# An attention block, forward and backward: the key cache read once instead of twice, through a per-head V^T(e·K), and the work around it rescheduled

## The chip, the cores and the metric

The kernel runs on one core of one Trainium2 chip. The metric is the device time of one execution in microseconds (us). The engines are called by the names that the profile uses: PE (TensorE, matrix products; PEld is its weight load), DVE (VectorE), ACT (ScalarE), POOL (GpSimd) and SP (SyncE, which here only issues DMA).

## The reference

One transformer block with an adaptive layer norm, for a single decoded token per batch entry, and its full vector-Jacobian product. Batch is 2, there are 32 heads, so 64 (batch, head) pairs, called heads below. All data is bf16.

```python
# per head: q is one vector of 128; K and V are 8192 x 128
scores = einsum('bhqd,bhkd->bhqk', q, k_cache) * Dh ** -0.5
p = softmax(scores)
o = einsum('bhqk,bhkd->bhqd', p, v_cache)
x = x + ga * (o @ wo)                     # then layer norm, SwiGLU FFN (512 -> 1376 -> 512), residual
...
_out, _vjp = jax.vjp(_f, A_x, A_k_cache, A_v_cache, A_wq, A_wo, B_w1, B_w3, B_w2, c, w_mod)
return (_out, *_vjp(grad_out))
```

What matters is the size of things. K and V hold 134.2 MB each (64 heads of 2.10 MB), and their gradients dK and dV are as large. With one query per head, the gradients are outer products:

- dV[k,:] = p[k] · dO, and dK[k,:] = ds[k] · q · scale, where dP[k] = V[k,:] · dO, ds[k] = p[k] · (dP[k] − σ) and σ = o · dO.
- dq = scale · Σ ds[k] · K[k,:].

dO is known only after every head's output has gone through the output projection, the FFN and back. So any scheme has at least two passes over the heads: one before the FFN, one after.

## The kernel before

It makes three passes over caches. Pass 1 reads K: 64 transposes and 64 one-column products per head give the scores of all heads. Then one batched softmax in fp32. Pass 2 reads V: 64 one-column products per head give o. After the FFN, pass 3 reads V and K again, one head after another:

```python
def c_load(i):
    d["v"] = vpool2.tile([P, KK, P], BF16, name="v2")           # two buffers
    nc.sync.dma_start(d["v"][:], A_v_cache[b, h]...)
    d["k"] = kpool2.tile([P, KK, P], BF16, name="k2")           # one buffer
    nc.sync.dma_start(d["k"][:], A_k_cache[b, h]...)
# ... cut: c_prep_dp transposes V (64 blocks, evicted by ACT) and gets DP = V dO, 64 one-column products
def c_finish(i):
    nc.vector.scalar_tensor_tensor(dscs32[:], DP_ps[:], SIG32[:, h, b:b + 1], p32, ALU.subtract, ALU.mult)
    # ... cut
    for kk in range(KK):                                        # KK = 64 rows of 128 per partition
        nc.vector.tensor_scalar(dk_sb[:, kk, :], Qb[:], dscs32[:, kk:kk + 1], None, ALU.mult)
        if kk % 8 in (1, 4, 7):
            nc.scalar.activation(dv_sb[:, kk, :], DOb[:], ACT.Copy, scale=p32[:, kk:kk + 1])
        else:
            nc.vector.tensor_scalar(dv_sb[:, kk, :], DOb[:], p32[:, kk:kk + 1], None, ALU.mult)
    nc.gpsimd.dma_start(out_2[b, h]..., dk_sb[:])
    nc.scalar.dma_start(out_3[b, h]..., dv_sb[:])
    for kk in range(KK):                                        # dq, the only reason to read K again
        nc.tensor.matmul(misc[:, 2 * P:2 * P + 1], k_sb[:, kk, :], dscs_bf[:, kk:kk + 1],
                         start=(kk == 0), stop=(kk == KK - 1))
```

The gradients of the weights follow as a tail of their own.

Of the kernel before, what the change touches and what calls it, by code (L numbers as in the profile page):

```python
# [12 lines left out]
AX = mybir.AxisListType  # L13
EPS = 1e-5
# [3 lines left out]
def kernel(  # L18
# [29 lines left out]
    assert Sq == 1  # L48
# [9 lines left out]
    NBH = B * H  # L58
    SCL = float(Dh) ** -0.5
    GRP = 8  # L60
    assert KK % GRP == 0
    NSD = 0
    NSP = KK - NSD
    NGA = NSP // GRP
    NGC = KK // GRP
# [3 lines left out]

    cst = ctx.enter_context(tc.tile_pool(name="cst", bufs=1))  # L70
    cols = ctx.enter_context(tc.tile_pool(name="cols", bufs=1))
    estp = ExitStack()
    tpsum = estp.enter_context(tc.tile_pool(name="tpsum", bufs=3, space=bass.MemoryType.PSUM))
# [3 lines left out]
    identf = cst.tile([P, P], F32, name="identf")  # L77
    masks.make_identity(nc, identf[:])
    onesf = cst.tile([P, P], F32, name="onesf")
    nc.vector.memset(onesf[:], 1.0)  # L80
    eps_t = cst.tile([P, 1], F32, name="eps_t")
    nc.vector.memset(eps_t[:], EPS)

    P32_all = cst.tile([P, NBH, KK], F32, name="P32_all")
    O32 = cst.tile([P, H, B], F32, name="O32")
    O_bf = cst.tile([P, H, B], BF16, name="O_bf")
    qT32 = cst.tile([P, H, B], F32, name="qT32")
    qT_bf = cst.tile([P, H, B], BF16, name="qT_bf")
    DO32 = cst.tile([P, H, B], F32, name="DO32")
    DO_bf = cst.tile([P, H, B], BF16, name="DO_bf")  # L90
    DQ32 = cst.tile([P, H, B], F32, name="DQ32")
    DQ_bf = cst.tile([P, H, B], BF16, name="DQ_bf")
    SIG32 = cst.tile([P, H, B], F32, name="SIG32")
    wqT_bf = cst.tile([P, H, D], BF16, name="wqT_bf")
    wmT_bf = cst.tile([P, MC, D], BF16, name="wmT_bf")
# [3 lines left out]

    x_col = col("x_col")  # L100
    c_col = col("c_col")
    dy_col = col("dy_col")
    sigc_col = col("sigc_col")
    sc_col = col("sc_col")
    sc_col_bf = col("sc_col_bf", NC, BF16)
    dslc_col = col("dslc_col")
    mod_col = col("mod_col", MC)
    mean1 = col("mean1", 1)
    rstd1 = col("rstd1", 1)
    xn1_col = col("xn1_col")  # L110
    h1_col = col("h1_col")
    h1_col_bf = col("h1_col_bf", NC, BF16)
    attn_col = col("attn_col")
    x1_col = col("x1_col")
    mean2 = col("mean2", 1)
    rstd2 = col("rstd2", 1)
    xn2_col = col("xn2_col")
    h2_col = col("h2_col")
    h2_col_bf = col("h2_col_bf", NC, BF16)
    gate_col = col("gate_col", FC)  # L120
    up_col = col("up_col", FC)
    sigg_col = col("sigg_col", FC)
    sg_col = col("sg_col", FC)
    hh_col = col("hh_col", FC)
    hh_col_bf = col("hh_col_bf", FC, BF16)
    dsl_col = col("dsl_col", FC)
    ffn_col = col("ffn_col")
    x2_col = col("x2_col")
    d_gb_col = col("d_gb_col")
    d_ffn_col = col("d_ffn_col")  # L130
    d_ffn_col_bf = col("d_ffn_col_bf", NC, BF16)
    d_hh_col = col("d_hh_col", FC)
    d_gate_col = col("d_gate_col", FC)
    d_gate_col_bf = col("d_gate_col_bf", FC, BF16)
    d_up_col = col("d_up_col", FC)
    d_up_col_bf = col("d_up_col_bf", FC, BF16)
    d_h2_col = col("d_h2_col")
    d_cb_col = col("d_cb_col")
    d_xn2_col = col("d_xn2_col")
    d_x1_col = col("d_x1_col")  # L140
    d_ga_col = col("d_ga_col")
    d_attn_col = col("d_attn_col")
    d_attn_col_bf = col("d_attn_col_bf", NC, BF16)
    d_h1_col = col("d_h1_col")
    d_ca_col = col("d_ca_col")
    d_xn1_col = col("d_xn1_col")
    d_x0_col = col("d_x0_col")
    d_mod_col = col("d_mod_col", MC)
    d_mod_col_bf = col("d_mod_col_bf", MC, BF16)
    d_sc_col = col("d_sc_col")  # L150
    d_c_col = col("d_c_col")

    for t_ in (gate_col, up_col, d_hh_col):
        nc.vector.memset(t_[:], 0.0)

    def dram_row_to_col(dram2d, dst_col, wrk, cvt_pool):
        rowb = wrk.tile([B, D], BF16, name="rowb")
        nc.scalar.dma_start(rowb[:], dram2d)
        row32 = wrk.tile([B, D], F32, name="row32")
        nc.vector.tensor_copy(row32[:], rowb[:])  # L160
        ps = cvt_pool.tile([P, NC, B], F32, name="colps", tag="vps")
        for kc in range(NC):
            nc.tensor.transpose(ps[:, kc, :], row32[:, kc * P:(kc + 1) * P], identf[:B, :B])
        nc.scalar.copy(dst_col[:], ps[:])

    def col_to_row_bf(src_col, nch, sizes, row_pool, ps_pool, name):
        assert src_col.dtype == F32
        row = row_pool.tile([B, nch * P], BF16, name=name, tag=name)
        per = 4
        for c0 in range(0, nch, per):  # L170
            cn = min(per, nch - c0)
            ps = ps_pool.tile([B, per * P], F32, name="rowps", tag="rowps")
            for i in range(cn):
                fs = sizes[c0 + i]
                nc.tensor.transpose(ps[:, i * P:i * P + fs], src_col[:fs, c0 + i, :], identf[:fs, :fs])
            width = (cn - 1) * P + sizes[c0 + cn - 1]
            nc.vector.tensor_copy(row[:, c0 * P:c0 * P + width], ps[:, :width])
        return row

    def ln_forward(x_in_col, xn_out, mean_t, rstd_t, wrk, psum_pool):  # L180
        ps = psum_pool.tile([P, NC, B], F32, name="lnps", tag="vps")
        nc.tensor.matmul(ps[:], onesf[:], x_in_col[:], start=True, stop=True)
        s1 = wrk.tile([P, 1, B], F32, name="ln_s1")
        nc.vector.tensor_reduce(s1[:, 0, :], ps[:].rearrange("p kc b -> p b kc"), AX.X, ALU.add)
        nc.scalar.mul(mean_t[:], s1[:], 1.0 / D)
        xc = wrk.tile([P, NC, B], F32, name="ln_xc")
        nc.vector.tensor_tensor(xc[:], x_in_col[:], mean_t[:].to_broadcast((P, NC, B)), ALU.subtract)
        sq = wrk.tile([P, NC, B], F32, name="ln_sq")
        nc.vector.tensor_mul(sq[:], xc[:], xc[:])
        ps2 = psum_pool.tile([P, NC, B], F32, name="lnps2", tag="vps")  # L190
        nc.tensor.matmul(ps2[:], onesf[:], sq[:], start=True, stop=True)
        s2 = wrk.tile([P, 1, B], F32, name="ln_s2")
        nc.vector.tensor_reduce(s2[:, 0, :], ps2[:].rearrange("p kc b -> p b kc"), AX.X, ALU.add)
        std = wrk.tile([P, 1, B], F32, name="ln_std")
        nc.scalar.activation(std[:], s2[:], ACT.Sqrt, bias=eps_t[:], scale=1.0 / D)
        nc.vector.reciprocal(rstd_t[:], std[:])
        nc.vector.tensor_mul(xn_out[:], xc[:], rstd_t[:].to_broadcast((P, NC, B)))

    def ln_backward(g_col, xn_col, rstd_t, out_col, wrk, psum_pool, add_col=None):
        gx = wrk.tile([P, NC, B], F32, name="lnb_gx")  # L200
        nc.vector.tensor_mul(gx[:], g_col[:], xn_col[:])
        both = wrk.tile([P, NC, 2, B], F32, name="lnb_both")
        nc.vector.tensor_copy(both[:, :, 0, :], g_col[:])
        nc.vector.tensor_copy(both[:, :, 1, :], gx[:])
        ps = psum_pool.tile([P, NC, 2, B], F32, name="lnbps", tag="vps")
        nc.tensor.matmul(ps[:], onesf[:], both[:], start=True, stop=True)
        ss = wrk.tile([P, 1, 2, B], F32, name="lnb_ss")
        nc.vector.tensor_reduce(ss[:, 0, :, :], ps[:].rearrange("p kc t b -> p t b kc"), AX.X, ALU.add)
        nc.scalar.mul(ss[:], ss[:], 1.0 / D)
        t1 = wrk.tile([P, NC, B], F32, name="lnb_t1")  # L210
        nc.vector.tensor_tensor(t1[:], g_col[:], ss[:, :, 0, :].to_broadcast((P, NC, B)), ALU.subtract)
        t2 = wrk.tile([P, NC, B], F32, name="lnb_t2")
        nc.vector.tensor_mul(t2[:], xn_col[:], ss[:, :, 1, :].to_broadcast((P, NC, B)))
        nc.vector.tensor_tensor(t1[:], t1[:], t2[:], ALU.subtract)
        nc.vector.tensor_mul(out_col[:], t1[:], rstd_t[:].to_broadcast((P, NC, B)))
        if add_col is not None:
            nc.vector.tensor_add(out_col[:], out_col[:], add_col[:])

    esq = ctx.enter_context(ExitStack())
    kpool = esq.enter_context(tc.tile_pool(name="kpool", bufs=3))  # L220
    heads = [(b, h) for b in range(B) for h in range(H)]
    NHD = len(heads)
    k_tiles = {}

    def k_load(i):
        b, h = heads[i]
        k_tiles[i] = kpool.tile([P, KK, P], BF16, name="k_sb")
        nc.sync.dma_start(k_tiles[i][:], A_k_cache[b, h].rearrange("(p kk) d -> p kk d", p=P))
# [7 lines left out]
    for i in range(min(3, NHD)):  # L236
        k_load(i)
# [534 lines left out]
```

## Time and profile before

The first four runs had a median of 2263.3 us (2243.78 to 2266.1). The profiled execution spans 2262.2 us. First, lines of the page of the kernel before: busy time of each engine with its share of the span, then the span in 40 slices (a digit is the busy share in tenths; PEclk is the granted TensorE clock; GB/s is what the DMA engines moved).

```profile
...
PE 1344.2 (59%) x26590; PEld 1192.6 (53%) x26590; DVE 1408.7 (62%) x7399; ACT 1341.3 (59%) x2847; POOL 35.2 (2%) x72
...
DVE  1444444620000058888788788788788788788775
...
PEclk9999999865555566556656656565656665656555
DMA  6999999579999849999999999999999999999975
GB/s 279 353 357 352 359 354 356 225 293 416 426 425 424 367 184 410 409 407 384 413 398 390 400 400 382 407 407 395 403 393 397 402 400 392 410 388 404 401 279 233
DMA packets 72041, 841.19 MB, mean 372 GB/s; under 512 B 7535, under 2 KB 18491, under 8 KB 21563
...
```

No engine is above 62%, and DMA is near full in most slices. But averages over stages hide limits, so the table by stage matters more. Next, the windows view of the kernel before: for each stretch its length, the busy time of PE, PEld, DVE, ACT and POOL (with instruction counts), the PE clock, the DMA share and GB/s.

```profile
...
25.00:415.00 390.00, 355.76 (x8190) 342.50 (x8191) 181.53 (x301) 256.20 (x291) 0.00 (x0) 1.00 0.90 341
415.00:520.00 105.00, 62.11 (x1226) 56.79 (x1224) 43.86 (x75) 40.57 (x71) 0.00 (x0) 0.66 0.67 257
520.00:790.00 270.00, 101.48 (x3482) 97.00 (x3480) 13.82 (x81) 12.59 (x81) 0.00 (x0) 0.50 0.98 415
790.00:845.00 55.00, 42.91 (x802) 39.42 (x799) 25.45 (x130) 22.28 (x50) 0.00 (x0) 0.62 0.52 193
845.00:2165.00 1320.00, 711.18 (x12470) 631.66 (x12470) 1084.44 (x6646) 964.36 (x2260) 33.61 (x63) 0.62 0.97 397
2165.00:2262.00 97.00, 70.18 (x432) 24.73 (x432) 58.89 (x164) 44.01 (x96) 0.53 (x1) 0.50 0.64 254
...
```

| stretch | what runs | what limits |
|---|---|---|
| 25–415 | keys, scores | PE 355.8 of 390 us busy at full clock; DMA 0.90 |
| 415–520 | softmax, weight transposes | nothing is full |
| 520–790 | values, o | DMA 0.98 at 415 GB/s |
| 790–845 | FFN | latencies |
| 845–2165 | gradients: 20.6 us a head | DMA 0.97 at 397 GB/s; DVE at 1084/1320 |
| 2165–2262 | weight gradients | nothing is full |

The gradient pass is 58% of the time. What fills DVE there is seen in the groups (line, engine, operation, output<-inputs, shapes, count, then busy us and mean ns of one, then idle time before it and what ended it), kernel before:

```profile
...
L610 DVE TENSOR_SCALAR dk_sb<-Qb,dscs 128x128 bf16<-128x128 bf16 x4096 | 677.1, 247 | 2.2
L588 ACT COPY vt<-tpv 128x1024 bf16<-128x1024 bf16 x512 | 488.4, 1032 | 9.5 <-PE tpv L586 3.9
...
L614 DVE TENSOR_SCALAR dv_sb<-DOb,P_all 128x128 bf16<-128x128 bf16 x2560 | 423.4, 247 | 235.8 <-DMA out_dram<-dv_sb 188.8 <-ACT rows L573 29.5 <-ACT dv_sb L612 14.3
...
```

4096 + 2560 multiplies of one 128x128 block have durations of 677.1 + 423.4 us. They overlap a little, so the busy time of DVE in the stage, 1084 us or 16.9 us a head, is the better figure. That is 82% of the 20.6 us, hidden below DMA as long as DMA needs more.

Finally the PE timeline of the key pass, kernel before (start, length, instruction group):

```profile
...
201.86 0.31 PE L288 MATMUL S_ps<-qT_bf,kt 128*128 128x1 bf16 x7
202.03 0.61 PE L305 MATMUL tpk<-identb,k_sb 128*128 128x128 bf16 x8
202.48 0.34 PE L288 MATMUL S_ps<-qT_bf,kt 128*128 128x1 bf16 x8
202.68 0.61 PE L305 MATMUL tpk<-identb,k_sb 128*128 128x128 bf16 x8
...
```

From the start of one set of 8 transposes to the start of the next, 0.65 us pass: 0.45 us for 8 transposes (56 ns each) and 0.20 us for 8 one-column products (25 ns each). These two spacings are the costs from which PE time of the new first pass can be built. The "length" column is no cost: a set of transposes is listed with 0.61 us, and the products behind it start 0.45 us after it.

### The profile page before, as it was taken

The numbers are of one execution on the slowest core, as the hardware profiler recorded it, in microseconds if no ns is written. First come the engines' busy times: TensorE is split into PE (matmuls) and PEld (weight loads), VectorE is DVE, ScalarE is ACT, GpSimd is POOL, SyncE is SP. The second block draws the span as 40 slices with busy tenths as digits, with TensorE's granted clock in tenths as the row PEclk, the third lists the DMA queues.
The fourth block names the chain that finished last, engine by engine and source line by source line (L and its number), as shares of the span: only waits on it lengthen the run. The fifth ranks groups of instructions, "written<-read, shape, count | busy, mean of one in ns | idle before, by whom it ended". The sixth has DMA issues, their size and how long they took to land.

```text
span 2262.2 us, 65422 instructions
## 1 busy us (share of the span) xinstructions
PE 1344.2 (59%) x26590; PEld 1192.6 (53%) x26590; DVE 1408.7 (62%) x7399; ACT 1341.3 (59%) x2847; POOL 35.2 (2%) x72
## 2 busy tenths in 40 slices
PE   3999999754333375555555555555455555455557
PEld 3888888644333375554444444444444444454431
DVE  1444444620000058888788788788788788788775
ACT  2666666620000047867767767767767777777754
POOL 0000000000000000000000000000000000000000
PEclk9999999865555566556656656565656665656555
DMA  6999999579999849999999999999999999999975
GB/s 279 353 357 352 359 354 356 225 293 416 426 425 424 367 184 410 409 407 384 413 398 390 400 400 382 407 407 395 403 393 397 402 400 392 410 388 404 401 279 233
DMA packets 72041, 841.19 MB, mean 372 GB/s; under 512 B 7535, under 2 KB 18491, under 8 KB 21563
## 3 DMA queue, kind: packets, MB, share of 16 engines
q1 hardware_dynamic: 45119, 553.72, 62.0%
q10 hardware_dynamic: 17404, 149.08, 15.7%
q0 software_dynamic: 9216, 134.22, 14.0%
q8 instruction: 208, 3.41, 0.6%
q14 instruction: 94, 0.77, 0.1%
HBM read 552.71 MB, written 284.28 MB: 370 GB/s over the span
## 4 chain that ended last, share of the span: by engine, by line
DMA 37%; ACT 26%; PE 20%; DVE 15%; issue 2%; ACTq 0%; DVEq 0%; SPq 0%
DMA out_dram<-dv_sb 23%; DMA v_sb<-in_A_v_cache_dram 11%; DVE dv_sb L614 10%; ACT vt L588 10%; ACT dv_sb L612 9%; PE tpk L305 7%; ACT kt L308 6%; PE S_ps L288 3%; DVE dk_sb L610 3%; PE o_ps L395 2%; PE bp L675 1%; DMA wo_sb<-in_A_wo_dram 1%; PE misc L574 1%; DMA rowb<-in_A_x_dram 1%; PE misc L575 1%
## 5 line engine op out<-in xcount | busy, mean ns | idle before, releaser
L610 DVE TENSOR_SCALAR dk_sb<-Qb,dscs 128x128 bf16<-128x128 bf16 x4096 | 677.1, 247 | 2.2
L614 DVE TENSOR_SCALAR dv_sb<-DOb,P_all 128x128 bf16<-128x128 bf16 x2560 | 423.4, 247 | 235.8 <-DMA out_dram<-dv_sb 188.8
L588 ACT COPY vt<-tpv 128x1024 bf16<-128x1024 bf16 x512 | 488.4, 1032 | 9.5 <-PE tpv L586 3.9
L586 PE MATMUL tpv<-identb,v 128*128 128x128 bf16 x4096 | 458.9, 279 | 13.3 <-DMA v<-in_A_v_cache_dram 13.3
L612 ACT ACTIVATE dv_sb<-DOb,P_all 128x128 bf16<-128x128 bf16 x1536 | 455.3, 393 | 0.2 <-ACT dscs_bf L606 0.2
L586 PEld LDWEIGHTS <-v 128*128 128x128 bf16 x4096 | 344.5, 125 | 14.0 <-DMA v<-in_A_v_cache_dram 13.7
L308 ACT COPY kt<-tpk 128x1024 bf16<-128x1024 bf16 x256 | 253.1, 1013 | 99.9 <-PE tpk L305 99.2
L305 PE MATMUL tpk<-identb,k_sb 128*128 128x128 bf16 x4096 | 293.3, 220 | 16.4 <-ACT kt L308 16.4
L310 DVE COPY kt<-tpk 128x1024 bf16<-128x1024 bf16 x256 | 177.0, 691 | 187.1 <-PE tpk L305 187.1
L591 PE MATMUL DP_ps<-DO_bf,vt 128*128 128x1 bf16 x4096 | 193.7, 168 | 96.3 <-ACT vt L588 91.5
L305 PEld LDWEIGHTS <-k_sb 128*128 128x128 bf16 x4096 | 236.1, 98 | 24.0 <-issue 23.9
L591 PEld LDWEIGHTS <-vt 128*128 128x128 bf16 x4096 | 177.1, 107 | 128.4 <-ACT vt L588 125.2
L395 PE MATMUL o_ps<-p_bf,v_sb 128*128 128x1 bf16 x4096 | 121.1, 165 | 182.9 <-DMA v_sb<-in_A_v_cache_dram 180.5
L577 ACT ACTIVATE Qb<-misc 128x128 bf16<-128x128 f32 x64 | 17.7, 277 | 343.2 <-PE misc L575 343.2
L618 PE MATMUL misc<-dscs_bf,k 128*128 128x1 bf16 x4096 | 116.5, 165 | 173.0 <-DMA k<-in_A_k_cache_dram 165.7
L395 PEld LDWEIGHTS <-v_sb 128*128 128x128 bf16 x4096 | 116.3, 104 | 187.9 <-DMA v_sb<-in_A_v_cache_dram 185.2
L570 PE MATMUL misc<-identf,qT 128*1 128x128 f32 x64 | 23.5, 373 | 320.6 <-DVE DQ L620 320.6
L618 PEld LDWEIGHTS <-k 128*128 128x128 bf16 x4096 | 112.0, 101 | 180.3 <-DMA k<-in_A_k_cache_dram 179.4
L570 PEld LDWEIGHTS misc<-identf,qT 128*1 128x1 f32 x64 | 5.2, 81 | 334.8 <-DVE DQ L620 334.7
L397 ACT COPY O<-o_ps 128x1 f32<-128x1 f32 x64 | 10.2, 159 | 271.8 <-PE o_ps L395 271.8
L288 PE MATMUL S_ps<-qT_bf,kt 128*128 128x1 bf16 x4096 | 162.8, 164 | 8.3
L288 PEld LDWEIGHTS <-kt 128*128 128x128 bf16 x4096 | 145.1, 96 | 14.3 <-ACT kt L308 13.7
(242 smaller groups left out, 786.0 us busy)
## 6 DMA issues: line engine op xcount, KB each, us to landing
k_sb<-in_A_k_cache_dram SPq DMA_DIRECT2D x64, 2048.0 KB
v_sb<-in_A_v_cache_dram SPq DMA_DIRECT2D x64, 2048.0 KB
v<-in_A_v_cache_dram SPq DMA_DIRECT2D x64, 2048.0 KB
k<-in_A_k_cache_dram SPq DMA_DIRECT2D x64, 2048.0 KB
out_dram<-dk_sb POOLq DMA_DIRECT2D x64, 2048.0 KB, 18.9
out_dram<-dv_sb ACTq DMA_DIRECT2D x64, 2048.0 KB
wq_sb<-in_A_wq_dram SPq DMA_DIRECT2D x1, 4096.0 KB
wo_sb<-in_A_wo_dram ACTq DMA_DIRECT2D x1, 4096.0 KB
```

What stands on the lines that cost most here:

```text
L288: nc.tensor.matmul(S_ps[:, cc:cc + 1], kt[:, j, :], qT_bf[:, h, b:b + 1], start=True, stop=True)
L305: nc.tensor.transpose(tp[:, j, :], k_sb[:, NSD + g * GRP + j, :], identb[:])
L308: nc.scalar.copy(kt[:], tp[:])
L310: nc.vector.tensor_copy(kt[:], tp[:])
L395: nc.tensor.matmul(o_ps[:], v_sb[:, kk, :], p_bf[:, kk:kk + 1], start=(kk == 0), stop=(kk == KK - 1))
L586: nc.tensor.transpose(tp[:, j, :], v_sb[:, g * GRP + j, :], identb[:])
L588: nc.scalar.copy(vt[:], tp[:])
L591: nc.tensor.matmul(DP_ps[:, cc:cc + 1], vt[:, j, :], DO_bf[:, h, b:b + 1], start=True, stop=True)
L610: nc.vector.tensor_scalar(dk_sb[:, kk, :], Qb[:], dscs32[:, kk:kk + 1], None, ALU.mult)
L612: nc.scalar.activation(dv_sb[:, kk, :], DOb[:], ACT.Copy, scale=p32[:, kk:kk + 1])
L614: nc.vector.tensor_scalar(dv_sb[:, kk, :], DOb[:], p32[:, kk:kk + 1], None, ALU.mult)
L618: nc.tensor.matmul(misc[:, 2 * P:2 * P + 1], k_sb[:, kk, :], dscs_bf[:, kk:kk + 1], start=(kk == 0), stop=(kk == KK - 1))
```

## The change

The intent is to read K once. If M = V^T(e·K), a 128x128 matrix per head with e the unnormalised softmax weights, is kept from the first pass, then dq = scale/Σe · (M^T dO − σ Σe·K) needs no K later. To build M while K and V are both present, they have to be loaded in the same pass, and the softmax has to be done per head in that pass. The rest of the change:

- e is stored with each weight twice, side by side (`E2`), and so is ds. Multiplies of 128x2048 elements then read a pair of weights with unit step in the innermost dimension, in place of one weight repeated along a row. dK and dV are made by eight such multiplies per head, in place of 128 small ones.
- 64 products of 129 columns per head build M and o at once; 32 one-column products with `u`, the sum of the two halves of a quarter of e·K, build Σe·K; four small GpSimd copies put e into column 129.
- K, V, dK, dV rotate through 10 shared buffers of 16 KB per partition; the V of two heads is kept over the FFN; all dK and dV stores are issued by GpSimd in halves of 1 MB.
- The weight gradients become tasks, one per slot of the last pass (a slot is a round of 8 of a head's 64 blocks). w_q and w_mod are read a second time for them (7 MB).
- The order of instructions on every engine is fixed by the program.

```diff
+def scale_k(i, q):                                   # a quarter of a head, QK = 16 of 64 blocks
+    t = ekp.tile([P, QK, 130], BF16, name="ek", tag="ek")
+    ks = slice(q * QK, (q + 1) * QK)
+    nc.vector.tensor_tensor(pair(t[:, :, 0:P], QK), pair(K[i][:, ks, :], QK),
+                            E2[:, i, ks, :].unsqueeze(2).to_broadcast((P, QK, P // 2, 2)), ALU.mult)
+    nc.gpsimd.tensor_copy(t[:, :, P:P + 1], E2[:, i, ks, 0:1])
+    u = ekp.tile([P, QK // 2, P], BF16, name="eh", tag="eh", bufs=2)
+    nc.vector.tensor_tensor(u[:], t[:, 0:QK // 2, 0:P], t[:, QK // 2:QK, 0:P], ALU.add)
+    # ... cut
+def mm_m(i, g):                                      # 8 of 64 blocks of V against those of e*K
+    # ... cut: m, t; kk = g * GRP + j; u, the sums of quarter g // 2
+    for j in range(GRP):
+        nc.tensor.matmul(m[:, 0:P + 1], V[i][:, kk, :], t[:, kk % QK, 0:P + 1], ...)
+    if g % 2 == 1:
+        for j in range(QK // 2):
+            nc.tensor.matmul(m[:, P + 1:P + 2], u[:, j, :], onesb[:], ...)
 # ... cut: the per-head chain row max -> transpose -> max -> broadcast -> Exp into E2
+def task_dq():
+    for i in range(NHD):
+        nc.tensor.matmul(ps[:, i:i + 1], M_all[:, i, :], DO_bf[:, h, b:b + 1], start=True, stop=True)
+    # ... cut
 # ... cut: last pass
-    d["k"] = kpool2.tile([P, KK, P], BF16, name="k2")
-    nc.sync.dma_start(d["k"][:], A_k_cache[b, h]...)
-    for kk in range(KK):
-        nc.vector.tensor_scalar(dk_sb[:, kk, :], Qb[:], dscs32[:, kk:kk + 1], None, ALU.mult)
-        # ... cut: dv_sb on ACT and DVE
+def outer(dst, n, which, w2, q):
+    nc.vector.tensor_tensor(pair(dst[:, ks, :], QK),
+        QD[n][:, which, :].rearrange("p (a b) -> p a b", b=2).unsqueeze(1).to_broadcast((P, QK, P // 2, 2)),
+        w2[:, ks, :].unsqueeze(2).to_broadcast((P, QK, P // 2, 2)), ALU.mult)
```

(A cut core of a diff that rewrites most of the kernel.)

## The prediction

> **What bounds the kernel now.** DMA. The page gives 841 MB at a mean 372 GB/s; PE, DVE and ACT are 59 to 62% busy. By stretches (busy times by window):
> - keys, 25 to 415 us: about 355 GB/s; PE 93% busy too (clock 1.0; timeline: 0.645 us per 8 transposes and 8 one-column products, 5.2 us a head).
> - softmax, weight transposes, to 520: DMA 0.60 to 0.85.
> - values, to 790: 415 GB/s; PE waits for loads (chain of waits).
> - feed-forward, to 845: DMA 0.52.
> - gradients, to 2165: 64 heads at 20.6 us, 8.4 MB each, 397 GB/s, DMA 0.97.
> - weight gradients, to 2262: 254 GB/s.
>
> **What the change does.** Keys and values come together; M = V^T(e*K) is kept per head, and dq comes from M, so K is read once: 134 MB go. Two V heads are kept (4 MB); w_q and w_mod are read again (7 MB). Estimate: 710 MB. Softmax becomes a per-head chain inside the first pass; the weight gradients are spread through the last, so the 97 us tail goes. All stores move to GpSimd's queue. Added per head in the first pass: PE 64 products 129 columns wide and 32 narrow ones; DVE four multiplies of 128x2048 bf16 and four adds of half that; GpSimd four small copies.
>
> **Costs per head.**
> First pass. PE at clock 1.0: 5.2 us as now, 64 at about 56 ns (spacing of transposes in the timeline), 32 at 25 ns: 9.6 us. DVE: the trace's fp32 tensor_tensor takes 4.41 us for 4096 elements. [...] ACT: six 1.01 us copies and small ones, 7 us. DMA: 4.2 MB, 10 us. Near-equal limits in lockstep: I take 11.3 us a head, 723 us, plus 25 start and 17 drain: 765 us (now 790 for the same loads plus softmax).
> Middle: exposed, with weight transposes that the value pass hid before: 60 us.
> Last pass: 2.1 MB in, 4.2 out per head, 15.5 us at 405 GB/s; [...] ACT 7 to 11, PE under 11 even at half clock. DMA binds: 64 x 15.5 plus 23 MB of weights and their gradients (57 us), ends 25: 1075 us.
>
> Sum 765 + 60 + 1075 = **1900 us**, range **1810 to 2010**. On the critical path lies the DMA time of the removed bytes (about 130 MB at 400 GB/s, 325 us) and most of the tail; the first pass gives little. Chances: faster by over 2% 0.94, within 2% 0.04, slower 0.02.
>
> **What would show it.** Total about 710 MB; last pass DMA share 0.95 or more, 400 to 415 GB/s, about 16 us a head; first pass 11 to 12 us a head, PE clock near 1.0, PE and DVE above 80%; [...] no tail.
>
> **What would make it wrong.** Multiplies at the single rate (2.2 us): DVE then needs 15 us a head first and 19 last, about 2250 in all. Lockstep waits between PE, DVE and ACT in the first pass (13 us a head adds 110). Too few 16 KB buffers, so that loads and stores wait on each other in the last pass. A first pass at DMA rate: 1830.

The sum came to 1900 us with all its terms. The first pass was taken as 11.3 us a head, 1.3 above DMA's 10, the largest of the near-equal terms; the last pass is DMA's 15.5 us a head. What the prediction calls the single rate is an estimate from the trace of the kernel before: 4.41 us for 4096 fp32 elements (TENSOR_TENSOR, L348 and L357) are 2.2 us for 2048. PE's "under 11 even at half clock" is an estimate too, twice the 5.2 us that it needs for 64 transposes and 64 one-column products at clock 1.0 in the key pass; 0.50 is the lowest granted clock in the windows view of the kernel before.

## The result, and the profile after

The kernel after has a median of 1825.79 us (1816.38 to 1831.52, 11 runs); the kernel before, in the same rounds and before them, 2262.58 us (2241.47 to 2266.1, 16 runs). The ratio is 0.8076, with a 95% interval of 0.8054 to 0.8097. Ratios here are the mean time of one kernel's runs over that of the other's of the same rounds, so they are not quite the ratio of the medians that are quoted. The outputs agree with the reference.

The page of the kernel after:

```profile
...
PE 1366.7 (75%) x24604; PEld 1264.3 (69%) x24604; DVE 1302.7 (72%) x1736; ACT 951.1 (52%) x1244; POOL 317.0 (17%) x557
...
DVE  2878888888888888567565665678777766677682
...
PEclk9999999999999999785556577587666555655675
DMA  9999999999999999079999999999999999999996
GB/s 387 414 415 400 402 385 394 389 410 384 391 389 380 386 394 371 16 288 416 412 413 420 415 417 415 411 414 418 418 420 419 419 417 417 419 417 414 418 410 265
DMA packets 79771, 709.33 MB, mean 390 GB/s; under 512 B 8160, under 2 KB 13644, under 8 KB 21932
...
```

132 MB are gone, and the mean rate rose from 372 to 390 GB/s. 841.19/372 and 709.33/390 give the two spans: 2261 and 1819 us. As arithmetic, the bytes make the larger share of the fall (132 MB at 372 GB/s are 355 us), the rate the smaller. But which part of the change made those bytes worth so much is not in this arithmetic.

The windows view of the kernel after, stage by stage, in the same columns:

```profile
...
18.00:740.00 722.00, 674.84 (x14582) 657.93 (x14579) 588.04 (x905) 417.81 (x575) 156.79 (x256) 0.99 0.97 388
740.00:789.00 49.00, 37.43 (x796) 36.48 (x797) 19.80 (x73) 20.18 (x26) 0.00 (x0) 0.71 0.27 94
789.00:1795.00 1006.00, 647.11 (x9105) 563.08 (x9103) 690.47 (x732) 508.15 (x638) 158.95 (x294) 0.63 1.00 413
1795.00:1819.00 24.00, 0.00 (x0) 0.00 (x0) 0.00 (x0) 0.00 (x0) 0.53 (x1) 0.50 0.32 133
...
```

| | before, us | after, us | difference |
|---|---|---|---|
| K and V once, softmax | 790 | 740 | −50 |
| FFN and its return | 55 | 49 | −6 |
| gradient pass and weight gradients | 1417 | 1030 | −387 |

A head of the last pass takes 15.4 us now ((1777.4 − 791.0)/64, from its first to its last product with dO), against 20.6, and the weight gradients are inside it: 24 us are left behind it. Its DMA is full (1.00 at 413 GB/s), DVE has 690 of 1006 us and PE runs at a granted clock of 0.63, unhurt. A head of the first pass takes 11.03 us ((723.9 − 18.2)/64, from the first to the last score product). There PE is 93% busy at clock 0.99 and DMA 0.97.

The groups of the kernel after that answer to L610 and L614 of before, and the new ones of the first pass:

```profile
...
L905 DVE TENSOR_TENSOR big<-QD,E 128x2048 bf16<-128x2048 bf16 x256 | 311.6, 1218 | 113.4 <-DMA out_dram<-big 82.2
...
L905 DVE TENSOR_TENSOR big<-QD,ds 128x2048 bf16<-128x2048 bf16 x256 | 311.9, 1220 | 94.2 <-PE tp L309 59.2
L342 DVE TENSOR_TENSOR ek<-big,E 128x2048 bf16<-128x2048 bf16 x256 | 311.0, 1215 | 41.5 <-issue 35.9
L357 PE MATMUL m_ps<-ek,big 128*128 128x129 bf16 x4096 | 328.3, 222 | 8.5 <-issue 6.1
...
L346 DVE TENSOR_TENSOR eh<-ek 128x1024 bf16<-128x1024 bf16 x256 | 177.3, 692 | 27.0 <-PE m_ps L362 5.0
...
```

Eight multiplies of 1.22 us per head replace 104 small DVE ones and 24 ACT ones: 9.8 us of DVE a head in place of about 17 (all of DVE's work in the last pass is 690 us, 10.8 a head). A multiply of 2048 bf16 elements per partition takes 1215 to 1220 ns in these groups; 2.2 us would be the time at the rate of the fp32 multiplies of the kernel before (4.41 us for 4096).

The GpSimd copies of 128x16 that put e into column 129 (L344, 256 of them, 642 ns on average) do not all take the same time. The 71 that started while one of the first pass's multiplies (L342) ran took 1259 ns on average and ended 0.11 us (median) after it; the 64 that started while DVE was idle took 250 ns. (Worked out from the starts and ends in the trace, which do not show why.)

The PE timeline of the kernel after, in the first pass:

```profile
...
66.67 0.61 PE L309 MATMUL tp<-identb,big 128*128 128x128 bf16 x8
67.11 0.34 PE L422 MATMUL s_ps<-qT_bf,kt 128*128 128x1 bf16 x8
67.31 0.63 PE L357 MATMUL m_ps<-ek,big 128*128 128x129 bf16 x8
67.78 0.34 PE L362 MATMUL m_ps<-onesb,eh 128*128 128x1 bf16 x8
67.98 0.61 PE L309 MATMUL tp<-identb,big 128*128 128x128 bf16 x8
68.43 0.32 PE L422 MATMUL s_ps<-qT_bf,kt 128*128 128x1 bf16 x7
69.61 0.16 PE L422 MATMUL s_ps<-qT_bf,kt 128*128 128x1 bf16 x1 [0.87 <-issue]
69.64 0.63 PE L357 MATMUL m_ps<-ek,big 128*128 128x129 bf16 x8
...
```

One round of 8 transposes, 8 score products, 8 wide products and, every second time, 8 narrow ones shows the costs of each set by the starts: 0.44, 0.20, 0.47 and 0.20 us. Eight rounds of a head make about 8 x (0.44 + 0.20 + 0.47) + 4 x 0.20 = 9.7 us of PE, worked out from this view. Before 69.61 PE is idle for 0.87 us, and the profile shows no releaser ("issue"); the experiments come back to it.

### The profile page after: what moved, and what is told of

It reads as the page before. It is cut to its first block, busy times and chain, and to the rows that moved or that the text cites. A ratio compares the mean times of both kernels' runs of the same rounds, so it can differ in the third digit from the quotient of the medians.

```text
span 1819.3 us, 55168 instructions
## 1 busy us (share of the span) xinstructions
PE 1366.7 (75%) x24604; PEld 1264.3 (69%) x24604; DVE 1302.7 (72%) x1736; ACT 951.1 (52%) x1244; POOL 317.0 (17%) x557
## 2 busy tenths in 40 slices
DMA packets 79771, 709.33 MB, mean 390 GB/s; under 512 B 8160, under 2 KB 13644, under 8 KB 21932
## 5 line engine op out<-in xcount | busy, mean ns | idle before, releaser
L314 ACT COPY kt<-tp 128x1024 bf16<-128x1024 bf16 x768 | 775.2, 1013 | 636.8 <-PE tp L309 617.7
L309 PE MATMUL tp<-identb,big 128*128 128x128 bf16 x8192 | 795.6, 255 | 24.3 <-DMA big<-in_A_k_cache_dram 9.3
L309 PEld LDWEIGHTS <-big 128*128 128x128 bf16 x8192 | 607.2, 114 | 110.4 <-issue 97.0
L905 DVE TENSOR_TENSOR big<-QD,E 128x2048 bf16<-128x2048 bf16 x256 | 311.6, 1218 | 113.4 <-DMA out_dram<-big 82.2
L968 PE MATMUL s_ps<-DO_bf,kt 128*128 128x1 bf16 x4096 | 196.2, 169 | 259.3 <-DVE kt L312 258.9
L968 PEld LDWEIGHTS <-kt 128*128 128x128 bf16 x4096 | 192.0, 110 | 279.0 <-DVE kt L312 278.2
L905 DVE TENSOR_TENSOR big<-QD,ds 128x2048 bf16<-128x2048 bf16 x256 | 311.9, 1220 | 94.2 <-PE tp L309 59.2
L342 DVE TENSOR_TENSOR ek<-big,E 128x2048 bf16<-128x2048 bf16 x256 | 311.0, 1215 | 41.5 <-issue 35.9
L357 PE MATMUL m_ps<-ek,big 128*128 128x129 bf16 x4096 | 328.3, 222 | 8.5 <-issue 6.1
L913 POOL DMA_DIRECT2D out_dram<-big x256 | 136.3, 532 | 834.1 <-DMA out_dram<-big 344.1
L344 POOL COPY ek<-E 128x16 bf16<-128x16 bf16 x256 | 156.8, 642 | 575.1 <-ACT E L335 381.9
L357 PEld LDWEIGHTS <-big 128*128 128x128 bf16 x4096 | 244.3, 98 | 16.7 <-issue 8.6
L422 PE MATMUL s_ps<-qT_bf,kt 128*128 128x1 bf16 x4096 | 177.9, 164 | 9.8 <-issue 8.3
L422 PEld LDWEIGHTS <-kt 128*128 128x128 bf16 x4096 | 158.4, 97 | 11.6 <-issue 9.9
L824 ACT COPY kt<-tp 128x1024 bf16<-128x1024 bf16 x28 | 28.9, 1032 | 5.4 <-PE m_ps L832 5.2
```

The costliest lines, as they stand in the source:

```text
L309: nc.tensor.transpose(tp[:, j, :], src[:, g * GRP + j, :], identb[:])
L314: nc.scalar.copy(kt[:], tp[:])
L342: nc.vector.tensor_tensor(pair(t[:, :, 0:P], QK), pair(K[i][:, ks, :], QK), E2[:, i, ks, :].unsqueeze(2).to_broadcast((P, QK, P // 2, 2)), ...
L344: nc.gpsimd.tensor_copy(t[:, :, P:P + 1], E2[:, i, ks, 0:1])
L357: nc.tensor.matmul(m[:, 0:P + 1], V[i][:, kk, :], t[:, kk % QK, 0:P + 1], start=(kk == 0), stop=(kk == KK - 1), skip_group_check=True)
L422: nc.tensor.matmul(S_ps[si][:, cc:cc + 1], kt[:, j, :], qT_bf[:, h, b:b + 1], start=True, stop=True)
```

## The experiments

**Theory at the start.** The removed K bytes are worth what they are because the last pass is limited by DMA alone; that in turn needs multiplies of the 1.22 us that they take in the kernel after, since at the old DVE cost of 17 us a head a last pass that moves 15 us worth of bytes could not show it. The first pass is limited by PE.
**Rivals.** (a) The gain is the removed bytes, which would have come in the old kernel as well. (b) The gain is DVE's and the schedule's, and the bytes count little. (c) For the first pass: not PE, but DMA, or the waits of the softmax chain, sets the 11 us.

Each call compared its kernels with runs of the kernel before on the same chip; medians of before lay between 2258.65 and 2262.0 us in all calls. The kernel after was not run again in them: a difference to its 1825.79 us compares two calls, so a few us of it mean nothing. (A DMA share in a view can come out slightly above 1: 1.01 in a_k_again, 1.02 in a_load8.)

### b_no_k2: only the K bytes removed, in the kernel before

```diff
-            d["k"] = kpool2.tile([P, KK, P], BF16, name="k2")
-            nc.sync.dma_start(d["k"][:], A_k_cache[b, h]...)
+            if i == 0:
+                k_once.append(kpool2.tile([P, KK, P], BF16, name="k2"))
+                nc.sync.dma_start(k_once[0][:], A_k_cache[b, h]...)
+            d["k"] = k_once[0]
```

dq is wrong (every head uses the K of the first).

> The kernel before, with the second reading of K left out of the last pass (one K tile is loaded once and used for every head, so dq is wrong on purpose); nothing else changes. Theory (the bytes of the second K reading are what the change takes off the critical path): the last pass loses 134 MB and its DMA need falls from 20.6 us to 6.3 MB at about 400 GB/s = 15.7 us a head, but VectorE is busy 1084 us in that pass, 16.9 us a head, so VectorE becomes the next limit at 17 to 17.5 us a head: about 2050 us in all, 710 MB. Rival (the last pass is held by producing the outer products on VectorE and ScalarE, and DMA is only busy beside it): within 2% of 2262 us.

Measured: 2065.15 us (2063.25 to 2069.56), ratio 0.917 (0.9119 to 0.9222): 195 us less than the kernel before (2259.85). The windows view of b_no_k2, its gradient pass, in the columns of before:

```profile
...
845.00:1968.00 1123.00, 688.01 (x12488) 615.83 (x12488) 1088.27 (x6666) 964.41 (x2262) 33.76 (x63) 0.64 0.91 351
...
```

The pass takes 1123 us, 17.5 us a head, in place of 1320. DVE is busy for 1088 us of it, 97%, and DMA has fallen to 0.91 and 351 GB/s. So in the old kernel the same bytes are worth 195 us, and no more, because DVE's own 17 us a head are next in line. Rival (a) falls: 242 us of the 437 are not to be had this way.

### a_k_again: the K bytes put back, in the kernel after

```diff
                     load(V, A_v_cache, order[n + 3]) if order[n + 3] not in V else None
+                load(K, A_k_cache, order[n])
```

The loaded K is not used; the result is right.

> The kernel after, with one more 2 MB load of K per head in the last pass, into a buffer that nobody reads. Theory (after the change the last pass is still bound by DMA): 134 MB at the 418 GB/s of that pass is 321 us more, about 2145 us, 844 MB. Rival (the last pass is now held by VectorE or by buffers, DMA has room): under 100 us more.

Measured: 2121.87 us (2116.86 to 2126.21), ratio 0.9418 (0.9365 to 0.9472), 296 us above the kernel after. The windows view of a_k_again, its last pass:

```profile
...
790.00:2080.00 1290.00, 634.29 (x8987) 548.55 (x8985) 675.44 (x718) 505.35 (x635) 156.16 (x289) 0.60 1.01 420
...
```

20.2 us a head, at 1.01 and 420 GB/s, with DVE at 675 of 1290 us. The last pass of the new kernel follows its bytes. The same 134 MB are worth 195 us in the one kernel and 296 us in the other. Rival (b) falls as well: bytes count, by more than in the old kernel. But this run shows the other part too. It moves 843.6 MB, as much as the kernel before (841.2), and is still 138 us faster than that kernel. So of the 437 us about 300 need the bytes to go, and about 140 come from the rest of the change at equal bytes: the weight gradients inside the last pass, the softmax inside the first, a DMA that rarely rests (399 GB/s on average, against 372). No run takes these apart.

### a_single: the pairing of the weights taken out, in the kernel after

```diff
-        nc.vector.tensor_tensor(pair(t[:, :, 0:P], QK), pair(K[i][:, ks, :], QK),
-                                E2[:, i, ks, :].unsqueeze(2).to_broadcast((P, QK, P // 2, 2)), ALU.mult)
+        nc.vector.tensor_tensor(t[:, :, 0:P], K[i][:, ks, :],
+                                E2[:, i, ks, 0:1].to_broadcast((P, QK, P)), ALU.mult)
```

and the same in `outer`. One weight is now repeated along the innermost dimension; the arithmetic and the result are the same.

> The kernel after, with every multiply by the weights reading one weight with an innermost step of zero in place of a pair of equal weights; the same arithmetic and results. Theory [...]: a multiply takes about 2.25 us in place of 1.22; VectorE then needs about 14 us a head in the first pass and 19.5 in the last, so about 940 + 50 + 1250 = 2240 us. Rival (VectorE has room, or the pairing does not matter): multiplies stay at 1.22 us, or the time stays within 2% of 1826 us.

(The 2.25 us stand as an estimate: by the 4.41 us for 4096 fp32 elements in the kernel before, 2048 take 2.2 us.)

Measured: 2278.79 us (2276.56 to 2280.56), ratio 1.0115 (1.006 to 1.0171). The groups of a_single:

```profile
...
L905 DVE TENSOR_TENSOR big<-QD,ds 128x2048 bf16<-128x2048 bf16 x256 | 584.7, 2285 | 2.1
...
L342 DVE TENSOR_TENSOR ek<-big,E 128x2048 bf16<-128x2048 bf16 x256 | 584.0, 2281 | 39.0 <-issue 36.6 <-ACT E L335 2.4
...
```

and its windows view, first and last pass:

```profile
...
60.00:960.00 900.00, 715.24 (x13850) 687.62 (x13847) 823.88 (x860) 402.96 (x549) 268.08 (x246) 0.90 0.75 292
1030.00:2250.00 1220.00, 675.55 (x9089) 584.57 (x9088) 1213.79 (x725) 513.79 (x637) 157.27 (x291) 0.59 0.87 338
...
```

Every multiply takes 2.28 us in place of 1.22, DVE is busy 92% of the first stretch and 99% of the last, and DMA is no longer full in either. The whole gain of 437 us is gone, with the same 709 MB as the kernel after. A weight that is repeated is read with step 0 in the innermost dimension, a pair with step 1; apart from the views written for it, the multiply is the same, and with the repeated weight it takes 1.87 times as long. Only these two forms were run.

The two runs b_no_k2 and a_single together say that neither half of the change carries it: fewer bytes with the old multiplies end at DVE, and so do the new algorithm's multiplies at 2.28 us each. The old kernel with cheap multiplies and K read twice was not run; a_k_again is the nearest to it.

### a_no_narrow: the 32 narrow products per head left out, but one

```diff
-            for j in range(QK // 2):
+            for j in range(1 if g == NG - 1 else 0):
```

dq is wrong (the Σe·K term is nearly empty).

> The kernel after, with 31 of the 32 narrow products per head of the first pass left out (dq is wrong on purpose); VectorE and DMA keep all their work. Theory (the first pass is bound by TensorE, 95% busy there): 31 products at 25 ns are 0.8 us a head, 50 us in all, about 1775 us. Rival (DMA, share 0.98 to 0.99 there, binds the first pass): at most 10 us less.

Measured: 1787.78 us (1787.54 to 1791.01), ratio 0.794 (0.7888 to 0.7993), 38 us less than after; a head of the first pass takes 10.53 us. PE had 0.8 us a head less to do, but the head became only 0.5 us shorter. The reason is in the stretch from 60 to 660 us. The windows view there of the kernel after:

```profile
...
60.00:660.00 600.00, 568.15 (x12388) 554.49 (x12385) 502.15 (x768) 358.44 (x494) 132.20 (x220) 0.99 0.99 394
...
```

and of a_no_narrow:

```profile
...
60.00:660.00 600.00, 544.95 (x11225) 533.91 (x11226) 526.74 (x807) 375.31 (x519) 133.31 (x231) 0.99 1.00 413
...
```

DMA had 0.99 in the one and 1.00 in the other, yet it moves 394 and 413 GB/s. A DMA share of 0.99 did not mean that DMA was giving all it could. At 413 GB/s, 64 heads of 4.19 MB and the 8.4 MB of w_o and FFN weights that this pass loads as well need (268.4 + 8.4)/413 = 670 us, 10.5 us a head. The 413 GB/s are those of this run, so the sum alone proves nothing; but they are also what the last pass of the kernel after reaches with DMA full (413), and the value pass of the kernel before came to 415. So a_no_narrow sits on the DMA limit, or very near.

### a_half_v: half the V bytes of the first pass, in the kernel after

```diff
-            nc.tensor.matmul(m[:, 0:P + 1], V[i][:, kk, :], ...
+            nc.tensor.matmul(m[:, 0:P + 1], V[i][:, kk % (KK // 2), :], ...
```

with loads of 32 of 64 rows to match, for all heads but the two kept. Its output is wrong, which doesn't matter for the time.

> The kernel after, loading only half of each V tile in the first pass and using that half twice (results wrong on purpose; the last pass loads V whole as before). 64 MB fewer bytes in the first pass. Theory (TensorE binds the first pass): the first pass keeps its length although DMA falls to a share of about 0.75 there, so the time stays within 12 us of 1826. Rival (DMA, share 0.98 to 0.99 there, binds or co-binds): 30 us less or more.

Measured: 1790.96 us (1788.71 to 1793.36), ratio 0.7923 (0.79 to 0.7945), 35 us less than after, 10.56 us a head. I had expected no change, because I held PE to be the limit and DMA to be no worse than close. The windows view of a_half_v:

```profile
...
60.00:660.00 600.00, 588.82 (x13002) 577.23 (x13000) 526.13 (x807) 375.23 (x518) 149.82 (x230) 1.00 0.81 307
...
```

DMA is down to 0.81, and PE is now busy 588.8 of 600 us. So this is what PE needs with its chain: 10.56 us a head. The theory that PE alone limits the first pass fell. Each of the two limits, alone, gives 10.5 to 10.6 us; both together give 11.03.

### a_few_mm: two wide products of eight

```diff
-        for j in range(GRP):
+        for j in range(0, GRP, GRP - 1):
```

Its output is wrong, which doesn't matter for the time.

> The kernel after, with 16 of the 64 wide products per head of the first pass kept (dq and the forward outputs are wrong on purpose). Theory (TensorE binds the first pass at about 10.8 us a head, and DMA comes next at 4.2 MB over about 415 GB/s = 10.1 us): TensorE drops to about 7 us a head, the first pass goes to DMA's 10.1 us and no further, so 40 to 50 us less, about 1780 us, DMA at 412 to 420 GB/s there. Rival (near-equal limits in lockstep, with VectorE at 10 us a head holding it too): 10.5 us a head or more, under 25 us less.

Measured: 1796.06 us (1794.04 to 1796.4), ratio 0.7943 (0.7922 to 0.7964), 30 us less than after, between what the two sides expected. The windows view of a_few_mm:

```profile
...
60.00:660.00 600.00, 507.62 (x10121) 485.74 (x10122) 520.11 (x797) 371.35 (x513) 149.85 (x228) 0.83 1.00 408
...
```

PE does far less and the head still takes 10.65 us: DMA is at 1.00 and 408 GB/s, as in a_no_narrow. But the granted clock fell to 0.83, and PE waits of 61 us for the row maxima appear (2.3 us in the kernel after), so this run changes three things at once and settles little by itself.

### a_no_adds: the four half-size adds per head left out

```diff
-        u = ekp.tile([P, QK // 2, P], BF16, name="eh", tag="eh", bufs=2)
-        nc.vector.tensor_tensor(u[:], t[:, 0:QK // 2, 0:P], t[:, QK // 2:QK, 0:P], ALU.add)
```

The narrow products read half of the rows instead. This makes Σe·K wrong; the outputs still pass the comparison with the reference, since that term is small here. So the comparison can't be relied on for this term.

> The kernel after, with the four half-size adds per head of the first pass left out; the narrow products read the unadded tile (dq is wrong on purpose). TensorE and DMA keep all their work. Theory (TensorE binds, VectorE only follows): VectorE loses 2.5 us a head, the time stays within 10 us of 1826. Rival (VectorE, 84% busy and in lockstep with TensorE, sets part of the 10.8 us): 25 us less or more.

Measured: 1817.16 us (1814.22 to 1820.89), ratio 0.8039 (0.8014 to 0.8064), 9 us less. DVE's busy time in the stretch fell from 502 to 366 of 600 us, and a head from 11.03 to 10.93. DVE, at 84%, is not a limit of the first pass.

### a_chain_late: more slack for the softmax chain

```diff
-    MOFF = NG + LAG + 5
+    MOFF = NG + LAG + 6
-        for off, f in ((0, chain_rowmax), (1, chain_t), (2, chain_b)):
+        for off, f in ((0, chain_rowmax), (3, chain_b)):
-        u = t - (NG + LAG + 3)
+        u = t - (NG + LAG + 4)
```

with the transpose of the row maxima moved behind the wide products of its slot.

> The kernel after, with the per-head maximum chain of the first pass given more room: its transpose goes behind the wide products of its slot, its broadcast and exponential come one slot later, and scaling and wide products start one slot later (a correct kernel, meant to be faster). Theory (TensorE binds the first pass, and about 0.5 us a head of it is waiting for the chain's small VectorE steps): 0.3 to 0.6 us a head less, until DMA's 10.1 us stops it, so about 1795 to 1805 us. Rival (the waits are only shifted): within 8 us of 1826.

Measured: 1824.95 us (1820.36 to 1826.96), ratio 0.8069 (0.804 to 0.8098): no change, correct. The waits of the chain do not set the head's 11 us: giving them more room changed nothing (in the kernel after, PE waits only 2.3 of 600 us for the row maxima).

### a_load4, a_load8, a_load4_chain: where do the PE pauses come from?

In the timeline of the kernel after, PE stood still at 69.6 us with "issue" as the reason, which means that the profile knows none. The DMA queue that the profile calls "instruction" (q8) had a piece in flight there: it started at 67.1 us and took 1.07 us, so PE went on 1.5 us after it had landed. The DMA view of the kernel after has that queue (packets, MB, share of 16 engines):

```profile
...
q8 instruction: 192, 3.15, 0.7%
...
```

In the trace PE has 49283 instructions (49208 matmuls and weight loads, and 75 of its sequencer); 192 pieces for these are one per 256. The kernel before has 53202 and 208, again one per 256, so I take the queue to carry the instructions of PE. I therefore listed, for the window of 60 to 660 us, all pauses of PE (more than 0.3 us from the start of one matmul to that of the next) and those which ended within 2 us after an instruction piece landed. The pieces are packets of 16,384 bytes, one every 6.2 us, so about a third of pauses would fall so by chance.

| kernel | pauses (sum, us) | of them after a piece (sum, us) | us a head |
|---|---|---|---|
| after | 58 (42.2) | 47 (33.3) | 11.03 |
| a_no_adds | 48 (36.3) | 47 (32.1) | 10.93 |
| a_chain_late | 47 (45.1) | 46 (39.0) | 11.07 |
| a_no_narrow | 57 (64.0) | 16 (15.6) | 10.53 |
| a_half_v | 53 (19.7) | 24 (10.1) | 10.56 |
| a_few_mm | 129 (115.9) | 38 (34.9) | 10.65 |

(Not a view of the profile: worked out from the starts of the matmuls and the packets of the instruction queue in the traces.) In the kernel after, and in the two runs that did not relieve PE or DMA, most pauses follow a piece (47 of 58, 47 of 48, 46 of 47). In those that did, the share falls to between 28 and 45%.

The traces say more than when. Number the pieces, and number all 49283 instructions of PE, both in order of time. In the kernel after, PE passes from instruction 256n + 193 to 256n + 194, for some n, 97 times in the window. At 42 of these places it pauses, 31.7 us in all, and each time it goes on 1.2 to 1.6 us after piece n has landed. Where piece n landed more than 1.7 us before, it never pauses. The program's own rhythm is another one (two rounds have 112 matmuls and weight loads), and a fixed cost per piece would show at every place. So PE waits here for its instructions. a_no_adds and a_chain_late have 47 and 46 such pauses at the same places (32.1 and 39.0 us), a_no_narrow has 1 of 88 (1.0 us), a_half_v 6 of 102 (4.2 us). The 27.5 us between the kernel after and a_half_v are 0.5 us a head, as much as separates 11.03 from 10.56. (Worked out from the traces like the table.)

Why the pieces come late is another question. One takes about 1 us from start to landing in each of these runs (medians 0.96 to 1.02), so it starts late. A guess, which the next runs test: if the pieces are late because they stand behind long loads, shorter loads should help:

```diff
-        qd.dma_start(v, src[b, h].rearrange("(p kk) d -> p kk d", p=P))
+        for c in range(4 if first[0] else 1):                    # 8 in a_load8
+            n = KK // 4 if first[0] else KK
+            qd.dma_start(v[:, c * n:(c + 1) * n, :], src[b, h]...[:, c * n:(c + 1) * n, :])
```

a_load4_chain is a_load4 with the edit of a_chain_late.

> The kernel after, with every 2 MB load of K and V in the first pass cut into four loads of 512 KB (rows of 4 KB in place of 16 KB); same bytes, same engines' work, correct results. Theory ([...] in the kernel after 47 of the 58 TensorE pauses over 0.3 us between 60 and 660 us end 1.2 to 1.6 us after such a piece, 33 us in all): the piece waits less behind 4 KB packets, those pauses fall under 15 us, and the time to about 1795 to 1805 us. Rival one (the pauses have nothing to do with the length of the data packets): within 8 us of 1826. Rival two (smaller packets cost DMA rate, and DMA co-binds): slower by 10 us or more.

("Such a piece" is one of the instruction pieces above.)

> As the kernel with loads cut in four, but cut in eight of 256 KB (rows of 2 KB). Theory of the late instruction pieces: at least as good as the cut in four as far as the pauses go (under 15 us of them between 60 and 660 us), unless the smaller packets lower the DMA rate below the 398 GB/s that the first pass needs now; 1790 to 1815 us. Rival one: within 8 us of 1826. Rival two: slower than the cut in four by 15 us or more.

> Loads cut in four and the later maximum chain together; correct. Theory (two different TensorE waits: late instruction pieces, and 0.3 us a head for the chain, which shows only once the first is gone): about 10 to 15 us under the cut in four alone, about 1785 to 1790 us, where DMA at 10.1 us a head stops it. Rival (the chain costs nothing): within 5 us of the cut in four.

Measured, all correct: a_load4 1822.61 us (1818.77 to 1831.57), ratio 0.8075 (0.8052 to 0.8097), no change, and 52 of its 70 pauses (31.3 of 41.6 us) still follow a piece. a_load4_chain 1822.39 us (1818.86 to 1826.42), ratio 0.8062 (0.8041 to 0.8083), no change, 53 of 54 pauses. a_load8 1862.34 us (1853.25 to 1870.95), ratio 0.8239 (0.8214 to 0.8264), slower: with eight loads for each 2 MB, DMA only gives 364 GB/s at a share of 1.02 (398 in a_load4), and now PE waits for K itself. The waits view of a_load8 (who waits for what: us in total, times, longest), 60 to 660 us:

```profile
...
PE tp L313 <- DMA big<-in_A_k_cache_dram: 59.2, 40, 12.8
...
```

Loads of 512 KB in place of 2 MB left the pauses as they were, so the length of the loads is not why the pieces come late. That PE stops for a piece is read from the traces, place by place; no run took the pieces away, and what makes them start late stays open.

### a_fold: fewer narrow products, with the right result

If PE and DMA are equal limits, PE must lose work to let DMA reach 413 GB/s, without losing the result. The narrow products can be halved by one more add on DVE, which has room when ACT takes over its evictions:

```diff
+        if q % 2 == 1:
+            nc.vector.tensor_tensor(u[:], u[:], eh.pop((i, q - 1))[:], ALU.add)
-        if g % 2 == 1:
+        if g % 4 == 3:
             u = eh.pop((i, g // 2))
-            kts[(i, g)] = transposes(K[i], g, g in (2, 6))
+            kts[(i, g)] = transposes(K[i], g, False)
```

> The kernel after, with the half sums of two neighbouring quarters added once more on VectorE, so that 16 of the 32 narrow products per head of the first pass fall away, and with the two evictions per head that VectorE did there moved to ScalarE, which is 60% busy; correct results, meant to be faster. Theory (TensorE is the first limit of the first pass; leaving out 31 narrow products took 38 us off): half of those products, 0.4 us a head, about 18 to 25 us less, 1800 to 1808 us; VectorE's load is unchanged (1.3 us of adds for 1.4 us of evictions). Rival (ScalarE at 8.9 us a head and the longer VectorE chain take it back): within 8 us of 1826.

Measured: 1807.44 us (1802.64 to 1808.31), ratio 0.7999 (0.7966 to 0.8032), correct; 18 us less than after, 10.78 us a head. The windows view of a_fold:

```profile
...
60.00:660.00 600.00, 561.31 (x11800) 547.51 (x11798) 525.24 (x789) 465.08 (x618) 154.48 (x224) 0.99 1.00 404
...
```

DMA moves 404 GB/s, half way between 394 and 413. The pauses for instruction pieces are down to 7 of 92 (4.5 us), but another wait has grown. The waits view, 60 to 660 us, of the kernel after:

```profile
...
PE s_ps L325 <- DVE rm L319: 2.3, 14, 0.2
...
```

and of a_fold:

```profile
...
PE s_ps L325 <- DVE rm L319: 28.3, 53, 0.6
...
```

PE now waits 28.3 us for the row maxima. The edit of a_chain_late, which brought nothing to the kernel after, was not tried on top of a_fold.

a_fold is the fastest correct kernel, 1% below the kernel after. It was run at another time. The ranges of the two (up to 1808.31, from 1816.38) do not overlap.

## Why the prediction was right, and where its terms were off

The prediction was 1900 us, from 765 + 60 + 1075; measured were 1819 in the profile, from 740 + 49 + 1030, and 1826 as median. The direction and the size came out as said, with 0.94 on faster; the time lies near the low end of the range, 16 us above 1810.

- **"What bounds the kernel now. DMA."** Right for the gradient pass, with an omission. DVE with 17 us a head was hidden about 3 us below. b_no_k2 shows it as the limit the moment that K goes.
- **"Estimate: 710 MB."** 709.33 measured.
- **"DMA binds" in the last pass, about 16 us a head, share 0.95 or more, 400 to 415 GB/s.** Share 1.00, 413 GB/s, 15.4 us; a_k_again shows that it follows bytes. The term of 1075 us is the one furthest off, by 45 us. It put 1049 us at 405 GB/s, which are 425 MB, plus 25 us. The stretch from 789 to 1795 us moved 415.5 MB (1006 us at 413 GB/s): 4.2 MB of kept V were named but not taken off, and 4.6 MB came already in the middle (49 us at 94 GB/s). The whole difference of 9.5 MB is 23 us, and 413 in place of 405 GB/s another 20 us. The 24 us behind it were predicted as 25.
- **"About 130 MB at 400 GB/s, 325 us" for the removed bytes.** Measured by putting the bytes back: 296 us. In the kernel before they were worth 195 us. The sum was made per stage and so had the interplay with DVE inside, but the sentence about the critical path gave the bytes a worth of their own that they do not have: with the old multiplies they are worth 195 us in the old kernel (b_no_k2), and with multiplies of 2.28 us the time of the new one is that of DVE (a_single).
- **"Most of the tail".** It went: 97 us before, 24 after. The work of it is inside the last pass, which is at its DMA limit anyway.
- **First pass, 11.3 us a head, PE and DVE above 80%, clock near 1.0, "the first pass gives little".** 11.03 us, PE 95% and DVE 84% from 60 to 660 us, clock 0.99, and 50 us in all. 17 of the 25 us that the term was too high are 64 x 0.27 us, the rest is the start (18 us, not 25). "Near-equal limits in lockstep" was right in kind: a_no_narrow and a_half_v show 10.5 to 10.6 us with either limit relieved, and 0.5 us lost where there are both, about what PE's waits for its instructions come to. The 11.3 was no sum but a margin of 1.3 us over the largest term of 10, so that it came within 0.3 us is partly luck. Which of the near-equal ones count was not said, and the waits that it feared, "between PE, DVE and ACT", are not the ones: a_no_adds and a_chain_late moved little or nothing. The pair is PE and DMA.
- **"A first pass at DMA rate: 1830."** The median of 1826 us is close to it by luck. The first pass took 740 us, not the 695 that this case supposes (765 less 70); the rest came off the last pass and the middle.
- **"Multiplies at the single rate (2.2 us) ... about 2250 in all".** They take 1.22 us, and a_single, where they take 2.28 us, took 2279 us. The failure that the prediction named was real and was the one that mattered most.
- **"Exposed ... 60 us" in the middle.** 49 us.
- **"Too few 16 KB buffers".** The groups show GpSimd store issues waiting behind earlier stores (L913, 344.1 us in all), but DMA stays at 1.00, so it cost nothing that could be seen.

What stays open: why instruction pieces come late in the first pass (PE waits about 32 of 600 us for them), and how the 140 us that the change gains at equal bytes divide among its parts.

## What to carry to other kernels

What a removed transfer was worth here was set by the engine that was next in line: the same 134 MB were worth 195 us where VectorE stood about 3 us a head below DMA, and 296 us where the multiplies had been made cheaper in the same change. So cost every engine per head after the change, and when the next limit is close, lower it in the same change. And where two limits are nearly equal, the busy share may not say which of them binds: DMA at 0.99 moved 394 GB/s in the kernel after, and 413 at 1.00 in a_no_narrow. Take some of either away and see what rate the other reaches. When PE pauses without a releaser, see whether the pauses recur at the same place of every 256 of its instructions: in the kernel after it paused at 42 of 97 such places, 31.7 us of 600, each time until 1.2 to 1.6 us after an instruction piece had landed.
